# A decode step of attention and MLP on one core: the first tile of wo with seven rows to a partition, the rest of its rows by smaller loads

## The chip, the cores and the metric

The kernel runs on one core of a Trainium2 chip. The metric is the device time of one execution in microseconds; before the change the median of three runs is 393.55 us (393.46 to 393.61). Beside the runs there is one profiled execution, whose instructions, DMA packets and clock were recorded.

## The reference

Eight sequences each decode one token through an attention layer with a cached window and an MLP, both modulated by a condition `c` (adaLN).

```python
B, Sq, D = 8, 1, 512
Hq, Hkv, Sk, Dh = 32, 8, 8192, 128
W = min(4096, max(256, Sk // 4))          # the last 2048 positions of the cache
mod = (_silu(c) @ w_mod).reshape(c.shape[0], 6, 1, -1)
sa, ca, ga, sb, cb, gb = (mod[:, 0], mod[:, 1], mod[:, 2], mod[:, 3], mod[:, 4], mod[:, 5])
h = _layernorm(x) * (1 + ca) + sa
q = (h @ wq) in 32 heads;  k, v = the last W rows of k_cache, v_cache, each for 4 heads
o = softmax(q k^T * Dh ** -0.5) v
x = x + ga * (o.reshape(B, 1, Hq * Dh) @ wo)
h = _layernorm(x) * (1 + cb) + sb
out = x + gb * (relu(h @ w1 + b1) ** 2 @ w2 + b2)
```

All numbers are float32. The K and V windows are 8 x 8 x 2048 x 128 values each, 64 MiB for K and as much for V; wq and wo have 8 MiB each, w_mod 6, w1 and w2 3.5 each.

## The kernel before, in words

Eight key heads are worked off one after the other. For each there are two tiles of keys (four sequences each) and two of values, 4 MiB each: 128 partitions with 32 KiB. A tile goes to one of four big slots (`home`, 128 x 32768 values). A fifth, smaller slot (`small`, 128 x 4096 values, 16 KiB to a partition) takes in turn the second part of w_mod, the first three tiles of wo and the second half of w1.

All large loads are issued by SP, in the order of the list `loads`. A load is issued when a slot of its size is free: `done(key)` frees a slot, and `pump` then goes down the list until the next load finds no slot. The loads are therefore strictly in the order of the list, and on SP's queue a load that waits holds up those behind it.

The steps of the main loop (`for s in range(N + PV_LAG + 1)`, N = 32) are written by hand and set the order on each engine. In a step, VectorE transposes parts of a K tile (`transposes`), TensorE forms scores (`scores`), and five steps behind it multiplies the probabilities with V (`weighted`). `soft_a` to `soft_g` are the softmax of a head, spread over two steps. When a head's values are done, `parts` and `gather` bring its output into columns: `gather` selects with two matmuls against `pick`, transposes, and writes `oT`, 128 x 8 x 32. Two key heads, which are eight query heads, fill `oT` once: head and sixteenth of the head dimension on the partitions (16 h + d // 8), d % 8 in the middle index. Then `project_o(j)` multiplies the eight slices of `oT` with the eight rows that each partition holds of the j-th wo tile (1024 rows), into `wo_ps`, in four column groups of 32 that are added up later. The last of the four wo tiles comes with half of w1 in a big slot (`tail`).

After the loop come the sum over the groups, the residual, the layer norm, w1, the squared ReLU and w2, whose load is cut in four so that its matmuls can follow the pieces. The inputs x and c (`xc`) and the biases come by small loads from ACT's queue. `small` is freed for the second wo tile by `project_o(0)`, at step 14 of the loop.

Of the kernel before, what the change touches and what calls it, by code (L numbers as in the profile page):

```python
# [8 lines left out]
F32 = mybir.dt.float32  # L9
# [10 lines left out]
def tile_adaln_cached_attention_mlp(  # L20
# [14 lines left out]
    nc = tc.nc  # L35
    P = 128
    B, HKV, SK, DH = k_cache.shape
    D = wq.shape[0]
    HQ = wq.shape[1] // DH
    REP = HQ // HKV  # L40
# [12 lines left out]
    consts = ctx.enter_context(tc.tile_pool(name="consts", bufs=1))  # L53
    work = ctx.enter_context(tc.tile_pool(name="work", bufs=2))
    ktp = ctx.enter_context(tc.tile_pool(name="ktp", bufs=2))
    ps_m = ctx.enter_context(tc.tile_pool(name="ps_m", bufs=2, space=bass.MemoryType.PSUM))
# [5 lines left out]
    xc_in = consts.tile([P, 2, P], F32, name="xc_in")  # L62
    x_in, c_in = xc_in[:, 0, :], xc_in[:, 1, :]
    nc.vector.memset(xc_in, 0.0)
    for q in range(D // P):
        b = slice(32 * q, 32 * q + B)
        for x, y in ((0, 2),) if q < 3 else ((0, 1), (1, 2)):
            nc.scalar.dma_start(xc_in[b, x:y], xc[b, x:y])

    ident = consts.tile([P, P], F32, name="ident")  # L70
    make_identity(nc, ident)
# [1 line left out]
    nc.gpsimd.memset(ones, 1.0)  # L73
    eps = consts.tile([P, 1], F32, name="eps")
    nc.vector.memset(eps, EPS)

    big = NJ * DH
# [7 lines left out]
    held = {}  # L87

    def size_of(key):
        return "small" if key[0] in ("wo", "w1") or key == ("mod", 1) else "big"  # L90

    def load(key):
        kind, i = key
        held[key] = free[size_of(key)].pop(0)
        if key == ("wq", 0):
            return
        t = slots[size_of(key)][held[key]]
        if kind in "KV":

            hk, c = divmod(i, 2)  # L100
            v = k_cache[4 * c : 4 * c + 4, hk] if kind == "K" else v_cache[c::2, hk]
            v = v[:, SK - W :, :].rearrange("u (p j) d -> p u (j d)", j=NJ)
            cuts = (0, big // 2, big) if key == ("V", 2 * HKV - 1) else (0, big)
            for x, y in zip(cuts, cuts[1:]):
                nc.sync.dma_start(t[:, x:y], v[..., x:y])
            return

        def rows(o, v):
            n = v.shape[1] * v.shape[2]
            nc.sync.dma_start(t[:, o : o + n].rearrange("p (a n) -> p a n", n=v.shape[2]), v)  # L110

        w1v = w1.rearrange("(p kc) n -> p kc n", p=P)

        def wo_rows(j):

            r = 2 * REP * DH
            v = wo[j * r : (j + 1) * r, :].rearrange("(p i) n -> p (i n)", p=P)
            nc.sync.dma_start(t[:, : big // 2], v)

        if kind == "wo":  # L120
            wo_rows(i)
        elif kind == "mod":

            v = w_mod.rearrange("(p kc) n -> p (kc n)", p=P)
            nc.sync.dma_start(t, v[:, big:] if i else v[:, :big])
        elif kind == "wq":

            o = base[held["wq", 0]]
            nc.sync.dma_start(home[:, o : o + 2 * big], wq.rearrange("(p k) n -> p (k n)", p=P))
        elif kind == "tail":  # L130
            wo_rows(HKV // 2 - 1)
            rows(big // 2, w1v[:, 0:2])
        elif kind == "w1":
            rows(0, w1v[:, 2:4])
        else:
            v = w2.rearrange("(p c) n -> p c n", p=P)
            for lo, hi in ((0, 8), (8, 12), (12, 13), (13, 14)):
                rows(D * lo, v[:, lo:hi])

    def slot(key, n, o=0):  # L140

        t = slots[size_of(key)][held[key]][:, o:]
        return t[:, : t.shape[1] // n * n].rearrange("p (a n) -> p a n", n=n)

    loads = [("mod", 0), ("mod", 1), ("wq", 0), ("wq", 1), ("K", 0), ("K", 1)]
    for n in range(2, 2 * HKV):
        if n in (4, 9, 13):
            loads.append(("wo", n // 4 - 1))
        loads += [("K", n), ("V", n - 2)]
    loads += [("V", 2 * HKV - 2), ("V", 2 * HKV - 1), ("tail", 0), ("w1", 0), ("w2", 0)]  # L150
    at = [0]
# [6 lines left out]
    def done(*keys):  # L158
        for k in keys:
            free[size_of(k)].append(held.pop(k))  # L160
        pump()
# [81 lines left out]
    for k in (2, 3, 4):  # L243
        n = 1 << k
# [134 lines left out]

    def soft_c(hk):  # L380
        pm = MX_.pop(hk)
        m1 = work.tile([1, 4, 32], F32, name="m1")
        nc.vector.tensor_reduce(
            m1.rearrange("p k (u r) -> p k u r", u=4),
            pm[0:1, :P].rearrange("p (u i r) -> p u r i", u=4, i=4)[:, None].to_broadcast([1, 4, 4, 8, 4]),
            axis=AX.X,
            op=ALU.max,
        )
        MX_[hk] = m1
# [78 lines left out]
    def gather(hk):  # L468

        o = OS_.pop(hk)  # L470
        b = slice(H * (hk % 2), H * (hk % 2) + H)
        pp = ps_m.tile([P, 512], F32, name="m_ps", tag="m_ps")
        for x in range(2):
            nc.tensor.matmul(  # L474
                pp[b].rearrange("p (d x e i) -> p x e d i", x=2, e=2, i=8)[:, x],
                pick[:, x].rearrange("p t u -> p (t u)"),
                o.rearrange("p e (d i) -> p e d i", i=8),
                start=True,
                stop=True,
            )  # L480
        tr = work.tile([P, 2, 8, 32], F32, name="tr", tag="b", bufs=1)
        nc.vector.transpose(  # L482
            tr[b].rearrange("p e i (x d) -> p (e i) x d", x=2),
            pp[b].rearrange("p (d x e i) -> p (e i) x d", x=2, e=2, i=8),
        )
        nc.vector.tensor_mul(
            oT[b, :, :B].rearrange("p i (w e) -> p e i w", e=2),
            tr[b, :, :, :4],
            RZ_[hk][b].rearrange("p (w e) -> p e w", e=2)[:, :, None, :].to_broadcast([H, 2, 8, 4]),
        )  # L490

    def project_o(j):

        last = j == HKV // 2 - 1
        key = ("tail", 0) if last else ("wo", j)
        w = slot(key, D)
        for i in range(8):
            nc.tensor.matmul(
                wo_ps[32 * (i % 4) : 32 * (i % 4) + 32, :],
                oT[:, i, :],  # L500
                w[:, i, :],
                start=(j == 0 and i < 4),
                stop=(last and i >= 4),
            )
        if not last:
            done(key)

    def late_tiles():

        late = work.tile([P, NJ, 8, 4], F32, name="pr4", bufs=1).rearrange("p j x w -> p (j x w)")  # L510
        rT = late[:, : FC * 32].rearrange("p (c b) -> p c b", b=32)
        b1_in, b2_in, x1, h2T = late[:NQ, 512 : 512 + FG], late[:NQ, 1024:1152], late[:, 1152:1280], late[:, 1280:1408]
        h2T = h2T.rearrange("p (c b) -> p c b", b=32)
        nc.gpsimd.memset(rT, 0.0)
        for t, v in ((b1_in, b1), (b2_in, b2)):
            v = v.rearrange("(g n) -> g n", g=NQ)
            for g in (0, 2):
                nc.scalar.dma_start(t[g : g + 2], v[g : g + 2])
        return rT, b1_in, b2_in, x1, h2T

    window(0)
# [2 lines left out]
    for s in range(N + PV_LAG + 1):  # L524
        g, i = divmod(s, C)
        q, h = divmod(s, 2)
        v = s - PV_LAG
        soft = 1 <= g <= HKV
        ends = v >= C and v % C == 0
        if i == 1 and soft and g < HKV:  # L530
            soft_e(g - 1)
        if s < N:
            transposes(q, 2 * h, 0)
        if 1 <= s <= N:
            scores((s - 1) // 2, 2 * ((s - 1) % 2) + 1)
            if i == 0:
                soft_a(g - 1)
        if s < N:
            transposes(q, 2 * h, 1)
        if i == 1 and soft:  # L540
            soft_f(g - 1)
        if v > C and v % (2 * C) == 1 and v < N:
            project_o(v // C // 2 - 1)
        if 1 <= v <= N:
            weighted(v - 1, 1)
        if i == 0 and soft:
            soft_b(g - 1)
        if s < N:
            transposes(q, 2 * h + 1, 0)
        if i == 1 and soft:  # L550
            soft_g(g - 1)
            if g == HKV:
                rT, b1_in, b2_in, x1, h2T = late_tiles()
        if i == 0 and soft:
            soft_c(g - 1)
        if 1 <= v <= N and v % 2 == 0:
            parts(v // 2 - 1)
        if s < N:
            scores(q, 2 * h)
        if i == 0 and soft:  # L560
            soft_d(g - 1)
            if g == HKV:
                soft_e(g - 1)
        if s < N:
            transposes(q, 2 * h + 1, 1)
        if 0 <= v < N:
            weighted(v, 0)
        if ends:
            gather(v // C - 1)
# [24 lines left out]

    pa = ps_m.tile([P, 512], F32, name="m_ps", tag="m_ps")
    nc.tensor.matmul(pa[:, 0:1], sel, x1sum, start=True, stop=True)
    xm = work.tile([P, P], F32, name="xm", tag="one_xm", bufs=1)
    nc.vector.tensor_mul(xm, x1, mul)
    nc.vector.tensor_add(xm, xm, add)
    nmean = work.tile([P, 1], F32, name="nmean")  # L600
# [40 lines left out]
    for f in range(FC):  # L641
        for q in range(NQ):
# [4 lines left out]
                start=False,  # L647
                stop=(f == FC - 1),
            )
    y = work.tile([P, P], F32, name="y", tag="one_y", bufs=1)  # L650
    nc.vector.tensor_mul(y, py[:, :P], modC)
    nc.vector.tensor_add(y, y, x1)
    nc.sync.dma_start(out, y)
# [36 lines left out]
```

## Time and profile before

| what | value |
|---|---|
| median of three runs | 393.55 us |
| the profiled execution | 393.74 us |
| its span, first to last instruction | 392.0 us |
| mean granted TensorE clock | 0.887 |
| busy: PE, VectorE (DVE), ACT, POOL | 253.9, 223.8, 46.2, 1.3 us |
| moved by DMA | 165.04 MB, mean 421 GB/s |

Busy time says how long an engine had an instruction in work; PE is TensorE's matmuls, PEld its weight loads, SP the engine that issues the large loads. DMA transfers are carried by 16 DMA engines; a queue (q1 is SP's, q10 ACT's, q8 and q14 bring instructions) is spread over them, and each transfer's rows are packets on them. A share of DMA is the mean over the 16. A row of the waits names who waited, for whom, the total, how often, and the longest. A row of the stretches has the stretch, its length, for each engine the busy time and the number of instructions, then TensorE's granted clock, the DMA share and the rate in GB/s. Times in the timeline and in the chain are from the start of the span.

### The profile page before, as it was taken

What the parts mean: (1) busy time and instruction counts of PE and PEld (TensorE: products, weight loads), DVE (VectorE), ACT (ScalarE), POOL (GpSimd) and SP (SyncE); (2) the same over time, 40 slices, a digit from 0 to 9 for tenths busy, and PEclk for the clock granted to TensorE, in tenths of its full rate; (3) what the DMA queues carried; (4) which work ended last, traced back from release to release, by engine and by line L of the source; (5) the groups of instructions that cost most, each with busy time, mean ns of one, the idle gap of its engine ahead of it and who ended that gap; (6) DMA issues with size and microseconds to landing.
All of it is one profiled execution on the core that took longest, in us unless ns stands there. A gap on an engine that the chain in (4) does not pass through costs nothing.

```text
span 392.0 us, 4698 instructions
## 1 busy us (share of the span) xinstructions
PE 253.9 (65%) x2020; PEld 77.0 (20%) x2020; DVE 223.8 (57%) x314; ACT 46.2 (12%) x89; POOL 1.3 (0%) x8
## 2 busy tenths in 40 slices
PE   0080959868327873797374828893774838996895
PEld 0030300112102221132121202220221211322333
DVE  1261199868057835784583817880786456855231
ACT  0120111310003100310031002010111003004010
POOL 0000000000000000000000000000000000000000
PEclk9996889998959995999698887998697959998999
DMA  8999999999999999999999999999999999999994
GB/s 329 423 468 419 433 431 431 431 430 411 443 428 428 426 428 431 436 435 433 433 430 428 431 430 431 430 428 433 415 441 431 430 431 433 429 416 428 424 420 172
DMA packets 6885, 165.04 MB, mean 421 GB/s; under 512 B 800, under 2 KB 976, under 8 KB 1232
## 3 DMA queue, kind: packets, MB, share of 16 engines
q1 hardware_dynamic: 6768, 164.69, 98.1%
q8 instruction: 16, 0.26, 0.3%
q10 hardware_dynamic: 96, 0.04, 0.0%
q14 instruction: 5, 0.04, 0.0%
HBM read 164.67 MB, written 0.07 MB: 420 GB/s over the span
## 4 chain that ended last, share of the span: by engine, by line
DMA 52%; DVE 23%; PE 19%; issue 4%; ACT 1%; SPq 0%; DVEq 0%; ACTq 0%
DMA home<-in_A_k_cache_dram 37%; DVE kT L191 12%; DMA home<-in_A_wq_dram 9%; PE s_ps L362 6%; DMA home<-in_B_w_dram 6%; DVE pT L428 5%; PE o_ps L448 4%; PE p_ps L393 3%; PE m_ps L307 2%; DVE pr L421 2%; DVE mx L376 1%; PE m_ps L378 1%; DVE qbd L325 1%; PE m_ps L474 1%; PE m_ps L398 1%
## 5 line engine op out<-in xcount | busy, mean ns | idle before, releaser
L191 DVE STREAM_TRANSPOSE kT<-home 128x1024 f32<-128x1024 f32 x128 | 151.5, 1220 | 82.5 <-DMA home<-in_A_k_cache_dram 77.2
L362 PE MATMUL s_ps<-kT,qst 128*32 128x512 f32 x512 | 129.1, 1075 | 21.3 <-DVE kT L191 21.0
L448 PE MATMUL o_ps<-home,pT 128*32 128x256 f32 x1024 | 69.8, 396 | 11.4 <-DVE pT L428 10.5
L448 PEld LDWEIGHTS o_ps<-home,pT 128*32 128x32 f32 x1024 | 33.5, 118 | 105.1 <-issue 65.2
L378 PE MATMUL m_ps<-ident,mx 128*1 128x128 f32 x16 | 4.3, 364 | 59.0 <-DVE mx L376 59.0
L362 PEld LDWEIGHTS s_ps<-kT,qst 128*32 128x32 f32 x512 | 14.2, 116 | 41.6 <-DVE kT L191 32.9
L428 DVE STREAM_TRANSPOSE pT<-pr 128x2048 f32<-128x2048 f32 x8 | 18.2, 2274 | 1.0 <-ACT pr L411 1.0
L411 ACT ACTIVATE pr<-pr,own 128x512 f32<-128x512 f32 x16 | 17.8, 1219 | 0.3
L405 ACT ACTIVATE pr<-p_ps,nm 128x512 f32<-128x512 f32 x8 | 5.5, 689 | 97.6 <-DVE nm L402 97.6
L372 ACT COPY ss<-s_ps 128x512 f32<-128x512 f32 x8 | 4.7, 587 | 101.0 <-issue 73.2
L350 ACT COPY qst<-q_ps 32x128 f32<-32x128 f32 x32 | 8.2, 257 | 70.5 <-PE q_ps L339 70.3
L307 PE MATMUL m_ps<-home,h1T 128*32 128x512 f32 x64 | 8.8, 713 | 9.8 <-DMA home<-in_A_wq_dram 9.8
L225 PE MATMUL m_ps<-xsum,sel 128*128 128x1 f32 x2 | 0.6, 364 | 19.7 <-DVE xsum L223 19.7
L378 PEld LDWEIGHTS m_ps<-ident,mx 128*1 128x1 f32 x16 | 0.7, 81 | 64.2 <-DVE mx L376 64.2
L325 DVE COPY qbd<-m_ps 32x128 f32<-32x128 f32 x8 | 3.0, 371 | 17.1 <-PE m_ps L322 17.0
L393 PE MATMUL p_ps<-ss,perm 128*128 128x512 f32 x16 | 12.5, 872 | 0.0
L402 DVE TENSOR_SCALAR nm<-m_ps 128x1 f32<-128x1 f32 x8 | 1.3, 158 | 17.1 <-PE m_ps L398 17.1
L474 PE MATMUL m_ps<-o_sb,pick 128*64 128x256 f32 x32 | 9.5, 424 | 0.9 <-DVE o_sb L466 0.9
L421 DVE TENSOR_SCALAR pr<-pr,own 128x512 f32<-128x512 f32 x16 | 9.2, 654 | 0.8 <-ACT pr L405 0.8
L203 DVE TENSOR_SCALAR e_sb<-e_sb 128x128 f32<-128x128 f32 x1 | 0.2, 226 | 14.4 <-ACT e_sb L202 14.4
L465 DVE TENSOR_SCALAR o_sb<-o_ps,bit 128x128 f32<-128x128 f32 x16 | 5.2, 328 | 5.3 <-PE o_ps L448 5.1
L482 DVE STREAM_TRANSPOSE tr<-m_ps 64x512 f32<-64x512 f32 x8 | 5.7, 714 | 4.4 <-PE m_ps L474 4.3
(124 smaller groups left out, 119.7 us busy)
## 6 DMA issues: line engine op xcount, KB each, us to landing
home<-in_A_k_cache_dram SPq DMA_DIRECT2D x16, 4096.0 KB, 27.3
home<-in_A_v_cache_dram SPq DMA_DIRECT2D x15, 4096.0 KB, 19.9
small<-in_A_wo_dram SPq DMA_DIRECT2D x3, 2048.0 KB
home<-in_w_mod_dram SPq DMA_DIRECT2D x1, 4096.0 KB, 12.6
home<-in_A_v_cache_dram SPq DMA_DIRECT2D x2, 2048.0 KB, 21.0
small<-in_w_mod_dram SPq DMA_DIRECT2D x1, 2048.0 KB
home<-in_A_wo_dram SPq DMA_DIRECT2D x1, 2048.0 KB, 24.7
home<-in_B_w_dram SPq DMA_DIRECT2D x1, 2048.0 KB
```

Source lines behind the costliest of these rows:

```text
L191: nc.vector.transpose(KTS[q, j][:, rows], k[:, rows, 32 * j : 32 * j + 32])
L307: nc.tensor.matmul(pqs[r][32 * g : 32 * g + 32, :], hT[:, kc, :], w[:, 4 * r + g, :], start=(kc == 0), stop=(kc == NQ - 1),)
L325: nc.vector.tensor_copy(qbd[b, 4 * r : 4 * r + 4, j].rearrange("p g (b t) -> p t g b", t=REP), pT_[b].rearrange("p (t g b) -> p t g b", t= ...
L350: nc.scalar.copy(own[b, :, :, i, 0], pq[b, :P].rearrange("p (c m t) -> p c m t", c=2, t=REP))
L362: nc.tensor.matmul(s_ps[0][32 * g : 32 * g + 32, :], qst[hk % 2][:, P * (4 * c + u) + 32 * j :][:, :32], kT[:, u], start=(c == 0 and j == ...
L378: nc.tensor.matmul(MX_[hk][0:1, :P], mx, ident, start=True, stop=True)
L393: nc.tensor.matmul(sp, perm, SS_.pop(hk), start=True, stop=True)
L411: nc.scalar.mul(X_[hk][..., w], pr, own[:, w : w + 1])
L421: nc.vector.tensor_scalar(X_[hk][..., w], pr, own[:, w : w + 1], None, op0=ALU.mult)
L428: nc.vector.transpose(PT_[hk].rearrange("p e j r -> p j e r"), X_.pop(hk).rearrange("p j x w -> p j (x w)"))
L448: nc.tensor.matmul(O_[n][32 * g : 32 * g + 32, : 2 * DH], PT_[hk][:, e, j : j + 2].rearrange("p j r -> p (j r)"), vt[:, j : j + 2, :].rear ...
L474: nc.tensor.matmul(pp[b].rearrange("p (d x e i) -> p x e d i", x=2, e=2, i=8)[:, x], pick[:, x].rearrange("p t u -> p (t u)"), o.rearrange ...
```

## The change

The first wo tile is cut in two. Of the 128 rows of each of its eight query heads, the first 112 go to the slot at the old place in the list, as seven rows to a partition (`wo_rows(0)`); the head's 16 groups lie on 16 partitions as before. The last 16 rows of each head, 128 rows in all, come with a new load kind `far` into the same slot, where the second wo tile was: 12 of the 16 as four rows each on partitions 32 y + 4 q + a (y the half of the heads, a the head in it, q the group of four rows), by two loads whose outer size is three; the other four, one row each, on every fourth partition from 3. POOL first clears five rows of the slot. The second wo tile moves two places of `n` back in the list.

`gather` puts the outputs of the first two key heads in the order that fits: two matmuls become four. `project_o(0)` multiplies seven slices, and then moves the eighth with four matmuls against `fsel`, a selection matrix made at the start, into `oX`. `far_rows`, at step 18, multiplies the five slices of `oX` with the five rows of `far`. Beside that, the last of the x and c loads is no longer cut in two, each bias comes in one load instead of two, and some working tiles share memory or have one buffer.

```diff
-        for x, y in ((0, 2),) if q < 3 else ((0, 1), (1, 2)):
-            nc.scalar.dma_start(xc_in[b, x:y], xc[b, x:y])
+        nc.scalar.dma_start(xc_in[b], xc[b])
...
+    fsel = consts.tile([P, 4, P], F32, name="fsel")
+    nc.gpsimd.memset(fsel, 0.0)
+    for y in range(2):
+        nc.gpsimd.tensor_copy(
+            fsel[:, :, 32 * y : 32 * y + 12].rearrange("p r (q a) -> p r q a", a=4),
+            ident.rearrange("p (y a r q) -> p y r q a", y=2, a=4, r=4)[:, y, :, :3],
+        )
+    oX = consts.tile([P, 5, 32], F32, name="oX")
...
             r = 2 * REP * DH
+            if j == 0:
+                v = wo[:r].rearrange("(h d) n -> h d n", d=DH)[:, :112].rearrange("h (g i) n -> h g (i n)", i=7)
+                nc.sync.dma_start(t[:, : 7 * D], v)
+                return
...
+        elif kind == "far":
+
+            nc.gpsimd.memset(t[:, : 5 * D], 0.0)
+            v = wo[: 2 * REP * DH].rearrange("(h d) n -> h d n", d=DH)
+            four = v[:, 112:124].rearrange("(y a) (q r) n -> y q a (r n)", y=2, r=4)
+            for y in range(2):
+                nc.sync.dma_start(t[32 * y : 32 * y + 12, : 4 * D], four[y])
+            nc.sync.dma_start(t[3:P:4, 4 * D : 5 * D], v[:, 124:])
...
-        if n in (4, 9, 13):
-            loads.append(("wo", n // 4 - 1))
+        if n == 9:
+            loads.append(("far", 0))
+        if n in (4, 11, 13):
+            loads.append(("wo", (4, 11, 13).index(n)))
...
-        for i in range(8):
+        for i in range(8 if j else 7):
...
+        if j == 0:
+
+            px = ps_m.tile([P, 512], F32, name="m_ps", tag="m_ps")
+            for r in range(4):
+                nc.tensor.matmul(px[:, 32 * r : 32 * r + 32], fsel[:, r], oT[:, 7, :], start=True, stop=True)
+            nc.scalar.copy(oX[:, :4], px[:, :P].rearrange("p (r b) -> p r b", b=32))
+            nc.scalar.copy(oX[:, 4], oT[:, 7, :])
...
+    def far_rows():
+
+        w = slot(("far", 0), D)
+        for r in range(5):
+            nc.tensor.matmul(wo_ps[32 * (r % 4) : 32 * (r % 4) + 32, :], oX[:, r], w[:, r, :], start=False, stop=False)
+        done(("far", 0))
...
-            for g in (0, 2):
-                nc.scalar.dma_start(t[g : g + 2], v[g : g + 2])
+            nc.scalar.dma_start(t, v)
...
+        if s == 18:
+            far_rows()
```

More of the change, by code (lines that the diff above doesn't have):

```diff
@@ L89, in size_of @@
     def size_of(key):
-        return "small" if key[0] in ("wo", "w1") or key == ("mod", 1) else "big"
+        return "small" if key[0] in ("wo", "w1", "far") or key == ("mod", 1) else "big"
     def load(key):
@@ L381, in soft_c @@
         pm = MX_.pop(hk)
-        m1 = work.tile([1, 4, 32], F32, name="m1")
+        m1 = work.tile([1, 4, 32], F32, name="m1", bufs=1)
         nc.vector.tensor_reduce(
@@ L473, in gather @@
         for x in range(2):
[L474 to L480, printed above, removed]
+            to = pp[b].rearrange("p (d x e i) -> p x e d i", x=2, e=2, i=8)[:, x]
+            cuts = [(to, o.rearrange("p e (d i) -> p e d i", i=8))]
+            if hk < 2:
+                cuts = [
+                    (to[..., :7], o[:, :, :112].rearrange("p e (d i) -> p e d i", i=7)),
+                    (
+                        to[..., 7].rearrange("p e (r q) -> p e r q", r=4),
+                        o[:, :, 112:].rearrange("p e (q r) -> p e r q", q=4),
+                    ),
+                ]
+            for dest, src in cuts:
+                nc.tensor.matmul(dest, pick[:, x].rearrange("p t u -> p (t u)"), src, start=True, stop=True)
         tr = work.tile([P, 2, 8, 32], F32, name="tr", tag="b", bufs=1)
@@ L596, in tile_adaln_cached_attention_mlp @@
     nc.tensor.matmul(pa[:, 0:1], sel, x1sum, start=True, stop=True)
-    xm = work.tile([P, P], F32, name="xm", tag="one_xm", bufs=1)
+    xm = work.tile([P, P], F32, name="xm", tag="one_h_sb", bufs=1)
     nc.vector.tensor_mul(xm, x1, mul)
@@ L649, in tile_adaln_cached_attention_mlp @@
             )
-    y = work.tile([P, P], F32, name="y", tag="one_y", bufs=1)
+    y = work.tile([P, P], F32, name="y", tag="one_e_sb", bufs=1)
     nc.vector.tensor_mul(y, py[:, :P], modC)
```

## The prediction

> **What bounds the kernel now.** I read the page first, for the share of each resource; then the chain that ended last and the waits, for who waits for whom; then stretches of the span, for the rate of the transfers and for how they end. Columns of the queue rows: packets, MB, share of 16 engines.
>
> ```profile
> span 392.0 us, 4698 instructions
> ...
> DMA  8999999999999999999999999999999999999994
> ...
> q1 hardware_dynamic: 6768, 164.69, 98.1%
> q8 instruction: 16, 0.26, 0.3%
> q10 hardware_dynamic: 96, 0.04, 0.0%
> ```
>
> SP's queue (q1) keeps the 16 DMA engines busy for 98.1% of the span. No compute engine comes near that. The waits and the last pieces of the chain (start, length, what) agree:
>
> ```profile
> DVE kT L191 <- DMA home<-in_A_k_cache_dram: 77.2, 13, 13.5
> ```
>
> ```profile
> 364.39 22.71 DMA home<-in_B_w_dram
> ...
> 387.15 1.76 PE m_ps L643 x48
> ...
> 388.93 0.30 DVE y L651
> ...
> 389.26 0.29 DVE y L652
> ```
>
> VectorE waits 77.2 us for keys, and the end hangs on the last pieces of w2: when they land, 1.8 us of matmuls, two VectorE operations and the store remain. The time is therefore set by the DMA engine that finishes last. The stretches at the end show that the 16 do not finish together (the last three columns are PE clock, mean busy share of the 16 engines, GB/s):
>
> ```profile
> 384.00:384.50 0.50, 0.00 (x0) 0.00 (x0) 0.00 (x0) 0.00 (x0) 0.00 (x0) 1.00 1.00 397
> 384.50:385.00 0.50, 0.21 (x8) 0.25 (x12) 0.00 (x0) 0.00 (x0) 0.00 (x0) 1.00 0.75 303
> 385.00:385.50 0.50, 0.50 (x28) 0.50 (x24) 0.00 (x0) 0.00 (x0) 0.00 (x0) 1.00 0.60 246
> 385.50:386.00 0.50, 0.50 (x28) 0.50 (x21) 0.00 (x0) 0.00 (x0) 0.00 (x0) 1.00 0.50 205
> ...
> 386.50:387.00 0.50, 0.24 (x11) 0.00 (x0) 0.00 (x0) 0.00 (x0) 0.00 (x0) 1.00 0.50 193
> 387.00:387.50 0.50, 0.35 (x12) 0.35 (x16) 0.00 (x0) 0.00 (x0) 0.00 (x0) 1.00 0.43 164
> 387.50:388.00 0.50, 0.50 (x28) 0.50 (x24) 0.00 (x0) 0.00 (x0) 0.00 (x0) 1.00 0.10 37
> 388.00:388.50 0.50, 0.50 (x22) 0.24 (x16) 0.00 (x0) 0.00 (x0) 0.00 (x0) 1.00 0.13 33
> 388.50:389.00 0.50, 0.36 (x8) 0.09 (x8) 0.07 (x1) 0.00 (x0) 0.00 (x0) 1.00 0.00 0
> ```
>
> The share falls from 1.00 to 0.50 by 385.5 and stays there until 387: eight engines, the early half, are done at about 385.3, and the other eight end up to 388.4. Yet every load of q1 gives all engines the same bytes. What differs is the instruction queue: 0.3% of 16 x 392 us is 18.8 us, or 1.2 us for each of its 16 packets; two on each of eight engines would be 2.4 us, near the lag seen. So at most some 1.5 us (388.4 less the middle of the two ends) can be won by evening out the engines.
>
> **How many engines carry a load.** The counts of packets tell it. q1 has 47 loads and stores of 128 rows, 6016 data packets; the other 752 are 16 per load, one from each engine that closes its part. q10 has five loads of 8 rows and four of 2, 48 data packets, and 48 closing ones: a load with an outer size of 8 or 2 runs on 8 or 2 engines. One engine's rate:
>
> ```profile
> 84.00:124.00 40.00, 23.43 (x190) 6.88 (x186) 20.50 (x24) 4.62 (x9) 0.00 (x0) 0.83 1.00 428
> 124.00:164.00 40.00, 27.27 (x210) 7.87 (x206) 25.73 (x32) 4.63 (x9) 0.00 (x0) 0.87 1.00 430
> 291.00:333.00 42.00, 26.23 (x188) 7.33 (x186) 23.57 (x27) 4.62 (x9) 0.00 (x0) 0.80 1.00 431
> ```
>
> At 430 GB/s an engine moves 26.9 KB (of 1000 bytes) per us.
>
> **The change, part by part.**
>
> The first wo tile moved 131,072 bytes on each of 16 engines, 4.87 us. Now its source view is 8 heads, 16 groups, 3584 values, while the SBUF side still has 128 partitions. Bounds: cut by the source's outer size it runs on 8 engines, 229,376 bytes each, 8.53 us; cut by the partitions, on 16, 114,688 bytes, 4.26 us. I take 8, since an outer size of 8 cannot be dealt out to 16, and q10's loads of 8 rows are the nearest row. The eight get 3.66 us more, the other eight 4.87 us less.
>
> The two loads of outer size three carry 12 pieces of 8192 bytes each. By the same reading three engines move four pieces of each load, 65,536 bytes, 2.44 us (the other bound, 12 engines: 0.61 us). The load on every fourth partition has outer size 8: four pieces of 2048 bytes per engine, 0.30 us.
>
> Sum: the eight get 3.66 + 0.30 = 3.96 us, three of them 2.44 more, 6.40 us; the others lose 4.87 us. Bytes in all are unchanged. Which half the eight are decides the rest, and no view names an engine. I take the early half: where the single packets, which no view prints, can be followed from one's end to the next one's start, q10's lie mostly on chains without instruction packets. That is thin, so the other half keeps a chance. The three then end at 385.3 + 6.40 = 391.7 instead of 388.4, which is **3.3 us later**. If the eight are the late half, it is the whole 6.40 us.
>
> [...]
>
> **Does a late engine's delay reach the end?** Only if the three never run dry.
>
> ```profile
> DMA to landing us min/median/max: 17.2/22.2/35.1
> ```
>
> That row is of the K and V loads. The whole ones take 4,194,304 bytes / 430 GB/s = 9.75 us, so most are issued long before an engine comes to them, 12 us at the median. Issues now move back with landings, by about 3.3 us, but the three engines' own queues by 6.4 us: they stay fed, and the delay is passed on in full. The relieved eight may run dry now and then, at no cost, since they end 8 us early.
>
> **The rest, hidden.** The order on SP, around the second wo tile; rows are line, operation, tiles, the destination's shape and what it waits for. Before:
>
> ```order
> L105 DMA home<-in_A_k_cache_dram 128x1x8192 [waits DMAHW3_49,DVE_49]
> L105 DMA home<-in_A_v_cache_dram 128x1x8192 [waits DMAHW4_49,PE_49]
> L118 DMA small<-in_A_wo_dram 128x4096
> L105 DMA home<-in_A_k_cache_dram 128x1x8192 [waits DMAHW5_49,DVE_49]
> L105 DMA home<-in_A_v_cache_dram 128x1x8192 [waits DMAHW6_49,PE_49]
> ```
>
> After, three loads stand there, behind a wait for POOL, and the tile goes four loads further back:
>
> ```order
> L112 DMA home<-in_A_v_cache_dram 128x1x8192 [waits DMAHW3_49,PE_49]
> L139 DMA small<-in_A_wo_dram 12x1x2048 [waits Pool_49]
> L139 DMA small<-in_A_wo_dram 12x1x2048
> L140 DMA small<-in_A_wo_dram 32x1x512
> L112 DMA home<-in_A_k_cache_dram 128x1x8192 [waits DMAHW4_49,DVE_49]
> ```
>
> All K and V loads behind wait with SP. The rows of before for that place, and the one memset on POOL:
>
> ```profile
> 170.11 1.92 PE L498 MATMUL wo_ps<-small,oT 128*32 128x512 f32 x16
> ...
> 178.82 0.53 SPq L105 DMA_DIRECT2D home<-in_A_v_cache_dram  x1
> ...
> 179.40 0.59 SPq L118 DMA_DIRECT2D small<-in_A_wo_dram  x1
> ...
> 181.15 0.54 SPq L105 DMA_DIRECT2D home<-in_A_k_cache_dram  x1
> ```
>
> ```profile
> 358.57 0.47 POOL L514 MEMSET pr<- 128x448 f32 x1 [357.12 <-DVE pT L428]
> ```
>
> The slot is free at 172.0; a memset of 2560 columns costs 0.47 x 2560/448 = 2.7 us, so POOL is done near 174.7, and SP comes there at 179.4. Two more issues of 0.6 us move the next K load by 1.2 us at most, within the slack above. If the memset took over 7 us, it would begin to eat that slack.
>
> On PE four small matmuls follow the seven of the first tile:
>
> ```order
> L524 MATMUL wo_ps<-small,oT 32x512 [waits DMAHW5_49,DVE_49]
> L524 MATMUL wo_ps<-small,oT 32x512 x6
> L535 MATMUL m_ps<-oT,fsel 128x32 [waits Pool_49]
> L535 MATMUL m_ps<-oT,fsel 128x32 x3
> L469 MATMUL o_ps<-home,pT 32x256 x8
> ```
>
> The eight there were:
>
> ```order
> L498 MATMUL wo_ps<-small,oT 32x512 [waits DMAHW6_49,DVE_49]
> L498 MATMUL wo_ps<-small,oT 32x512 x7
> L448 MATMUL o_ps<-home,pT 32x256 x8
> ```
>
> One fewer in the group, four small ones, five in far_rows and four more in the two gathers are 12 more; eight took 1.92 us, so 3 us in all, below 2 us at one place. PE is busy 27 of 40 us in these stretches, DMA all of them: no cost. Two copies on ACT and the fsel work on POOL hide in the same way. Merging the xc and the bias loads saves three issues on ACT, at places where nothing waits long: no gain. Without that cover it is 3 us, once.
>
> **Rivals.** (a) *Not slower: the first tile stays on 16 engines.* For it: its SBUF side has 128 partitions, like every load of q1. Then all engines save 0.61 us on it, the three end at 385.3 - 0.61 + 2.44 + 0.30 = 387.4, the late half at 387.8, and the time is 392.9. It decides if packets show 16 closers for this load; it would be over 0.2% faster if the late half's instruction packets also cost less, down to 392.0 at most by the 1.5 us above.
>
> (b) *Shared receivers.* The first tile's eight engines now also write partitions that other engines fill at full rate. If a group of partitions takes no more than one engine's 26.9 KB/us, two writers double 8.53 us, three treble it. Two: 8.53 more on the three engines, 396.9 + 8.5 = 405.4. Three, where the far rows add nothing: 385.3 + 3.96 + 17.06 = 406.3, 17.9 later, 411.5. Against it: no row of before shows two engines at one receiver. [...]
>
> (c) *The eight are the late half*: 393.55 + 6.4 = 399.9.
>
> **The numbers.** The profiled execution took 393.74 us, 0.19 above the median of 393.55; the difference is put on the median: 393.55 + 3.3 = **396.9**. Chances: forecast 0.38, (b) 0.27, (c) 0.05, (a) 0.30, of which 0.12 beyond 0.2% faster. So faster 0.12, within 0.2% 0.18, slower 0.70; 0.2%, 0.8 us, is about what a measurement of this kernel can tell from no change. The range runs from 392.6, just under (a), to 406.0, which takes in two writers; three, and a larger gain, are left out, together under 0.2. The forecast's own range is 396 to 398.
>
> **What would show it.** Right: q1 with 6072 data and 758 closing packets (50 transfers; 46 on 16 engines, then 8, 3, 3, 8), 6830 in all; at the end a share of 0.5 before 385, near 0.2 in the last 2 us. (a): 6838 packets and an end like that of before. (b): stretches near 100 to 125 us under 430 GB/s at a share of 1.00, and then a long tail with four engines. Wrong also if the transfers at the end are no longer what the last matmuls wait for.

## The result

The changed kernel took 414.62 us (median of 6 runs, 410.34 to 415.32) against 393.5 us (393.4 to 393.81) for the kernel before in the same rounds: a ratio of 1.0505, interval 1.0454 to 1.0557. That is 21.1 us slower, where 3.3 were predicted. The profiled execution took 414.56 us.

### The profile page after: what moved, and what is told of

It reads as the page before. It is cut to its first block, busy times and chain, and to the rows that moved or that the text cites. A ratio compares the mean times of both kernels' runs of the same rounds, so it can differ in the third digit from the quotient of the medians.

```text
span 412.8 us, 4752 instructions
## 1 busy us (share of the span) xinstructions
PE 257.7 (62%) x2044; PEld 79.7 (19%) x2044; DVE 223.9 (54%) x314; ACT 46.7 (11%) x91; POOL 4.5 (1%) x12
## 3 DMA queue, kind: packets, MB, share of 16 engines
q1 hardware_dynamic: 6830, 164.69, 97.6%
## 4 chain that ended last, share of the span: by engine, by line
DMA 61%; DVE 21%; PE 14%; issue 4%; SPq 0%; ACT 0%; DVEq 0%; ACTq 0%
DMA home<-in_A_k_cache_dram 40%; DVE kT L212 12%; DMA home<-in_A_wq_dram 9%; DMA home<-in_B_w_dram 6%; DMA home<-in_A_v_cache_dram 5%; PE s_ps L383 4%; DVE pT L449 4%; PE p_ps L414 2%; PE m_ps L328 2%; PE o_ps L469 2%; DVE pr L442 2%; DVE mx L397 1%; DVE qbd L346 1%; PE m_ps L399 1%; PE m_ps L419 1%
## 5 line engine op out<-in xcount | busy, mean ns | idle before, releaser
L212 DVE STREAM_TRANSPOSE kT<-home 128x1024 f32<-128x1024 f32 x128 | 151.3, 1220 | 102.3 <-DMA home<-in_A_k_cache_dram 97.3
L328 PE MATMUL m_ps<-home,h1T 128*32 128x512 f32 x64 | 10.0, 797 | 10.9 <-DMA home<-in_A_wq_dram 10.9
L506 PE MATMUL m_ps<-o_sb,pick 128*64 128x256 f32 (+2 forms) x40 | 9.5, 374 | 0.9 <-DVE o_sb L487 0.9
## 6 DMA issues: line engine op xcount, KB each, us to landing
home<-in_A_k_cache_dram SPq DMA_DIRECT2D x16, 4096.0 KB, 36.3
```

Source lines behind the costliest of these rows:

```text
L212: nc.vector.transpose(KTS[q, j][:, rows], k[:, rows, 32 * j : 32 * j + 32])
L328: nc.tensor.matmul(pqs[r][32 * g : 32 * g + 32, :], hT[:, kc, :], w[:, 4 * r + g, :], start=(kc == 0), stop=(kc == NQ - 1),)
L506: nc.tensor.matmul(dest, pick[:, x].rearrange("p t u -> p (t u)"), src, start=True, stop=True)
```

## The profile after

The page of the changed kernel, first its span, the rows of the DMA engines by slices of 10.3 us, and the queues (packets, MB, share of the 16 engines):

```profile
span 412.8 us, 4752 instructions
...
DMA  9999999999999899999999999999999999999993
GB/s 357 459 407 403 453 410 451 413 443 210 154 257 429 365 411 451 419 395 427 426 440 411 422 440 416 446 416 446 416 448 408 451 413 437 414 429 418 428 418 138
...
q1 hardware_dynamic: 6830, 164.69, 97.6%
q8 instruction: 16, 0.26, 0.3%
q10 hardware_dynamic: 80, 0.04, 0.0%
```

The busy share of the DMA engines is as high as before nearly everywhere. The GB/s row is not: in three slices, from about 93 to 124 us, it falls to 210, 154 and 257. The 6830 packets of q1 are the number that the prediction gave for loads on 8, 3, 3 and 8 engines. Stretches of the same kernel around those slices (the last three columns are PE clock, DMA share, GB/s):

```profile
80.00:95.00 15.00, 11.72 (x96) 3.46 (x100) 12.84 (x15) 1.88 (x5) 0.00 (x0) 0.89 0.99 422
95.00:100.00 5.00, 2.36 (x20) 0.35 (x12) 2.75 (x4) 0.00 (x0) 0.00 (x0) 1.00 1.16 185
100.00:105.00 5.00, 3.73 (x40) 1.23 (x40) 0.00 (x0) 0.59 (x1) 0.00 (x0) 1.00 1.10 169
105.00:110.00 5.00, 0.00 (x0) 0.00 (x0) 0.00 (x0) 0.00 (x0) 0.00 (x0) 0.60 0.91 149
110.00:115.00 5.00, 0.00 (x0) 0.00 (x0) 0.00 (x0) 0.00 (x0) 0.00 (x0) 0.50 1.13 176
115.00:120.00 5.00, 0.00 (x0) 0.00 (x0) 0.00 (x0) 0.00 (x0) 0.00 (x0) 0.50 0.83 151
120.00:125.00 5.00, 0.00 (x0) 0.00 (x0) 0.00 (x0) 0.00 (x0) 0.00 (x0) 0.50 0.97 413
125.00:160.00 35.00, 22.06 (x170) 6.68 (x170) 24.72 (x30) 4.05 (x8) 0.00 (x0) 0.83 0.97 411
```

For 25 us all 16 engines count as busy and move 149 to 185 GB/s, then 413 again. All compute engines stand still from 105 to 125 us, and TensorE's granted clock falls in that time from 1.00 to 0.60 and 0.50. The stretch is that of the first wo tile: in the records of the trace, its packets of 14,336 bytes lie from 94.9 to 120.7 us.

The issues of K loads (number, KB each, median us to landing), of the kernel before:

```profile
home<-in_A_k_cache_dram SPq DMA_DIRECT2D x16, 4096.0 KB, 27.3
```

Of the changed kernel, the same row, then the wait for keys and the last pieces of the chain:

```profile
home<-in_A_k_cache_dram SPq DMA_DIRECT2D x16, 4096.0 KB, 36.3
```

```profile
DVE kT L212 <- DMA home<-in_A_k_cache_dram: 97.3, 13, 33.5
```

```profile
382.04 25.84 DMA home<-in_B_w_dram
407.93 1.30 PE m_ps L684 x40
```

VectorE's wait for keys went from 77.2 to 97.3 us, 20.1 more, with the longest single wait 33.5 instead of 13.5. The median time from issue to landing of the K loads is no sign of the delay, though it too went up, from 27.3 to 36.3 us: the kernel below that has no slow stretch and takes 394.2 us shows 36.3 as well. The chain still ends on w2: its pieces land about 20.8 us later (the last group of matmuls starts at 407.93, before at 387.15), which is the growth of the span, 412.8 less 392.0. The end itself, in stretches of 4 us:

```profile
396.00:400.00 4.00, 4.00 (x23) 1.30 (x22) 1.52 (x6) 0.49 (x2) 0.00 (x0) 1.00 0.99 418
400.00:404.00 4.00, 3.91 (x28) 1.69 (x24) 1.68 (x5) 0.27 (x1) 0.00 (x0) 1.00 0.92 384
404.00:408.00 4.00, 2.58 (x70) 1.79 (x72) 0.00 (x0) 0.00 (x0) 0.00 (x0) 1.00 0.50 193
408.00:412.00 4.00, 1.65 (x48) 1.11 (x48) 0.58 (x2) 0.00 (x0) 0.00 (x0) 1.00 0.08 26
```

Between 404 and 408 us the share is 0.50, half of the engines at work. Predicted were four or fewer in a long tail: the other eight were to be done 8 us early. They are not, so they lost time too. POOL's clearing of the slot took about what the prediction gave it (row of the groups of instructions; busy us, mean ns, idle before):

```profile
L135 POOL MEMSET small<- 128x2560 f32 x1 | 2.2, 2232 | 189.5 <-PE wo_ps L524 189.5
```

## The experiments

Two theories stood at the start. **Shared receivers**: several DMA engines write into the same group of partitions, and the group's rate is divided among them (rival b). **The source**: the parts of wo that the eight engines read lie 256 KB apart, and that slows the reads. A third came up on the way: **eight engines** by themselves are the cause. Each diff is against the kernel named ahead of it.

### The first tile alone

Against the changed kernel:

```diff
-        if n == 9:
-            loads.append(("far", 0))
-        if n in (4, 11, 13):
-            loads.append(("wo", (4, 11, 13).index(n)))
+        if n in (4, 9, 13):
+            loads.append(("wo", n // 4 - 1))
...
-        if s == 18:
-            far_rows()
```

> The changed kernel without the far loads and far_rows (128 rows of the sum are left out), the second tile back at its old place; the first tile on eight engines stays. Both theories: the slow stretch of about 25 us near 95 to 120 us stays, the far loads' share (0.3 to 2.7 us) goes: 411 to 414.5 us. If the far loads matter more than that, it falls under 408.

Measured: 414.46 us (414.28 to 414.63), ratio 1.0527 (1.0508 to 1.0546), span 412.5. The loss is in the tile: 414.46 less 393.7 for the kernel before beside it is 20.8 us, and the runs of the changed kernel, 21.1 us slower at the median, lie further apart than the difference. The stretches of this kernel:

```profile
95.00:98.00 3.00, 3.00 (x28) 0.69 (x20) 2.01 (x4) 0.00 (x0) 0.00 (x0) 1.00 1.36 217
98.00:101.00 3.00, 0.55 (x4) 0.00 (x0) 0.97 (x1) 0.00 (x0) 0.00 (x0) 1.00 0.75 115
101.00:104.00 3.00, 2.37 (x20) 1.01 (x24) 0.00 (x0) 0.00 (x0) 0.00 (x0) 0.64 1.11 169
...
115.00:120.00 5.00, 0.00 (x0) 0.00 (x0) 0.00 (x0) 0.00 (x0) 0.00 (x0) 0.50 0.84 152
120.00:125.00 5.00, 0.00 (x0) 0.00 (x0) 0.00 (x0) 0.00 (x0) 0.00 (x0) 0.50 0.98 409
```

They are those of the changed kernel: the far loads and the later second tile have no part in the slow stretch.

### The source at another spacing

Against the kernel with the tile alone; the parts start 113 rows apart instead of 128:

```diff
-                v = wo[:r].rearrange("(h d) n -> h d n", d=DH)[:, :112].rearrange("h (g i) n -> h g (i n)", i=7)
+                v = wo[: 8 * 113].rearrange("(h d) n -> h d n", d=113)[:, :112].rearrange("h (g i) n -> h g (i n)", i=7)
```

> As the run of the tile alone, but the eight parts of the source begin 113 rows (226 KiB) apart instead of 128 rows (256 KiB); the same bytes, eight engines, the same partitions (the rows are the wrong ones). Shared receivers: as the tile alone, within 2 us, with the slow stretch. Sources in step at 256 KiB: the tile runs at full rate, 8.5 us on eight engines, which end 3.7 us later than before's early half: about 394 us, no stretch under 400 GB/s.

Measured: 414.31 us, ratio 1.0523 (1.0504 to 1.0542), span 412.2. Another spacing changes 0.15 us: the source theory falls, as far as the distance of the parts goes.

### The same number of engines, half the bytes, three ways to place them

Three kernels load half of the tile on eight engines, 114,688 bytes on each, and differ only in the partitions and in whether two loads or one fill them. If each engine takes one of the eight outer parts of a load, which is the author's estimate from the counts of packets, an engine fills twice four partitions in the first two and eight in a row in the third. Against the kernel with the tile alone:

```diff
-                nc.sync.dma_start(t[:, : 7 * D], v)
+                for y in range(2):
+                    nc.sync.dma_start(t[32 * y : 32 * y + 32, : 7 * D], v[:, 4 * y : 4 * y + 4])
```

> As the run of the tile alone, but only half of the tile is loaded, by two loads of outer size 8 to 32 partitions each, 0 to 31 and 32 to 63, source parts still 256 KiB apart (half of the tile's rows are left out). [...] Shared receivers: no slow stretch; eight engines carry 4.27 us in place of 4.87, the other eight nothing: the end comes 3 to 3.5 us sooner, 390.0 to 390.6 us. Sources in step: a slow stretch of half the length, about 10 to 12 us, over 400 us.

Measured: 393.62 us (393.41 to 393.86), ratio 1.0 (0.9991 to 1.0009). There is no slow stretch, and no gain of 3 us either; the end of its trace, below, shows why.

The twin of that kernel, the same two loads 64 partitions higher (half of the tile's rows are left out):

```diff
+                    nc.sync.dma_start(t[64 + 32 * y : 96 + 32 * y, : 7 * D], v[:, 4 * y : 4 * y + 4])
```

> [...] Shared receivers: two writers to each of eight groups of partitions for as long as the loads last: the two loads take 8.5 us at half rate, up to 12 us if it is as bad as in the full tile, in place of 4.3; the three engines that end last then end 4 to 7.5 us later than in the twin: 397.5 to 401 us, with 8 to 12 us of a stretch under 350 GB/s. If the number of engines or the source is the cause, or nothing in this form is, it equals the twin: 393.6 us.

Measured: 399.2 us (398.6 to 399.74), ratio 1.0139 (1.0126 to 1.0153), within what shared receivers gave. The stretches of this kernel:

```profile
95.00:98.00 3.00, 3.00 (x28) 0.67 (x20) 2.20 (x4) 0.00 (x0) 0.00 (x0) 1.00 1.25 268
98.00:101.00 3.00, 1.62 (x24) 0.68 (x24) 0.78 (x1) 0.00 (x0) 0.00 (x0) 1.00 0.86 178
101.00:104.00 3.00, 2.47 (x24) 0.54 (x16) 0.00 (x0) 0.59 (x1) 0.00 (x0) 1.00 1.05 245
```

One load to partitions 0 to 63 instead of two:

```diff
+                nc.sync.dma_start(t[:64, : 7 * D], v[:, :8])
```

> The same half of the tile, the same partitions 0 to 63 as in the first of these twins, the same rows and eight engines, but in one load of outer size 8 with eight rows for each (half of the tile's rows are left out). [...] Shared receivers: the eight run at half rate, 8.5 us in place of 4.3, the other eight are not touched: about 397 to 398 us, and the DMA rate in the stretch falls to some 325 GB/s (eight at half rate, eight at full). If the other eight slow down too, what is shared is not the receiver alone. [...]

Measured: 398.37 us (398.3 to 398.45), ratio 1.0119 (1.01 to 1.0137), a little over what was expected.

Stretches of the kernel with two loads to partitions 0 to 63, in the middle and at the end:

```profile
95.00:98.00 3.00, 3.00 (x36) 0.79 (x32) 2.73 (x4) 0.00 (x0) 0.00 (x0) 1.00 1.08 462
98.00:101.00 3.00, 3.00 (x32) 0.75 (x24) 0.00 (x0) 0.59 (x1) 0.00 (x0) 1.00 1.05 446
101.00:104.00 3.00, 0.01 (x2) 0.00 (x0) 0.00 (x0) 0.00 (x0) 0.00 (x0) 1.00 0.98 415
104.00:107.00 3.00, 0.00 (x0) 0.00 (x0) 0.00 (x0) 0.00 (x0) 0.00 (x0) 0.64 1.02 437
...
384.00:386.00 2.00, 2.00 (x50) 1.27 (x52) 0.20 (x1) 0.00 (x0) 0.00 (x0) 1.00 0.38 151
386.00:388.00 2.00, 1.58 (x60) 1.31 (x52) 0.00 (x0) 0.00 (x0) 0.00 (x0) 1.00 0.18 61
```

Of the kernel with one load to the same partitions:

```profile
95.00:98.00 3.00, 3.00 (x28) 0.65 (x20) 2.43 (x4) 0.00 (x0) 0.00 (x0) 1.00 1.17 252
98.00:101.00 3.00, 1.61 (x24) 0.68 (x24) 0.56 (x1) 0.00 (x0) 0.00 (x0) 1.00 1.00 224
101.00:104.00 3.00, 2.25 (x24) 0.55 (x16) 0.00 (x0) 0.59 (x1) 0.00 (x0) 1.00 0.94 226
104.00:107.00 3.00, 0.00 (x0) 0.00 (x0) 0.00 (x0) 0.00 (x0) 0.00 (x0) 0.97 0.95 371
```

The number of engines, the bytes and the source are the same in all three, and the first moves 415 to 462 GB/s from 95 to 107 us, its twin 178 to 268 and the third 224 to 252 from 95 to 104 us. So it is the placement that decides, where rival (b) looked for the loss. In the kernel with two loads to partitions 0 to 63 the tile's packets took 0.54 us, in its twin on partitions 64 to 127 1.11 us, and in the one load to partitions 0 to 63 1.09 us, each time with the other eight engines loading keys. Which partitions an engine fills in the loads of keys is not shown; the expected times rest on an assumption of the author's. The last two rows of the kernel with two loads to partitions 0 to 63 are its end: a share of 0.18, about three engines of 16, from 386 to 388. The other eight have 4.87 us less to carry, so three of the tile's eight must be among the late ones, and they hold the end where it was. Why these three, with 0.6 us less to carry themselves, do not end a little sooner is not shown.

What neither theory expected is the size of the rate. The kernel with one load to partitions 0 to 63 was to move some 325 GB/s, with the eight engines of the tile at half rate and the other eight untouched. It moved 224 and 226, half of everything. The single DMA packets in the records of the traces, which no view prints, say the same (median us, with the number of packets: all of the tile, and those of 32,768 bytes that start and end while the tile is being loaded):

| kernel | packets of the tile | packets of 32,768 bytes beside them |
|---|---|---|
| before | 0.61 (128, of 16,384 bytes) | 1.21 (15) |
| half tile, two loads, partitions 0 to 63 | 0.54 (64, of 14,336 bytes) | 1.22 (40) |
| half tile, two loads, partitions 64 to 127 | 1.11 (64) | 2.41 (41) |
| half tile, one load, partitions 0 to 63 | 1.09 (64) | 2.30 (30) |
| changed kernel | 1.58 (128) | 3.28 (60) |

The large packets belong to K loads, which have the form that they have in the kernel before. In the middle of each load on eight engines, 8 packets of the tile and 8 large ones are in flight at a time, so the large ones are those of the other eight engines. They slow down about as much as the tile's: by two in the slow half tiles, by 2.7 in the changed kernel, where the tile's packets take 2.9 times as long as at full rate.

How many engines write into a group of partitions at a time is an estimate: if a group's rate is divided evenly, 0.54, 1.11, 1.09 and 1.58 us stand for one, two, two and three writers. No view names an engine or the partition of a packet, so neither the groups nor their writers are seen. Why the K packets, at 2.30 to 3.28 us instead of 1.21, slow down with the tile's is not shown.

### The whole tile in two loads of 64 partitions

Against the kernel before; the first tile in two loads of 64 partitions, with all rows:

```diff
+            if j == 0:
+                for y in range(2):
+                    nc.sync.dma_start(t[64 * y : 64 * y + 64, : big // 2], v[64 * y : 64 * y + 64])
+                return
```

> The kernel before with its first tile, all 1024 rows, in two loads of 64 partitions each, outer size 64 on both sides, so that 16 engines carry each of them; nothing is left out. [...] Shared receivers: 9.7 us for the tile on all engines in place of 4.9: 398.4 us, and more if it is as bad as in the full tile on eight engines. If the small number of engines is the cause: no change, 393.5 to 394 us.

Measured: 400.66 us (400.26 to 402.06), ratio 1.0185 (1.0166 to 1.0203). Stretches of this kernel:

```profile
95.00:98.00 3.00, 2.20 (x16) 0.26 (x8) 2.58 (x4) 0.00 (x0) 0.00 (x0) 1.00 1.19 235
98.00:101.00 3.00, 1.41 (x16) 0.72 (x20) 0.00 (x0) 0.00 (x0) 0.00 (x0) 0.77 0.92 202
101.00:104.00 3.00, 3.00 (x32) 0.86 (x24) 0.00 (x0) 0.56 (x1) 0.00 (x0) 0.66 1.04 213
104.00:107.00 3.00, 0.19 (x4) 0.00 (x0) 0.00 (x0) 0.02 (x1) 0.00 (x0) 0.91 1.06 235
107.00:110.00 3.00, 0.00 (x0) 0.00 (x0) 0.00 (x0) 0.00 (x0) 0.00 (x0) 0.50 0.86 306
```

From 95 to 107 us they show 202 to 235 GB/s, with the bytes of the kernel before: half the rate again. The tile's 128 packets of 1.27 us at the median are some 163 us, 11 at a time in the 15 us of these stretches, where the loads on eight engines had 8 at a time; that 16 engines carry each load is not shown. With eight engines at full rate in the half tile on partitions 0 to 63 (0.54 us a packet), the number of engines is not the cause; that theory falls. These five stretches of 3 us moved 3.57 MB where 430 GB/s would have moved 6.45; 2.88 MB at 430 GB/s are 6.7 us, the loss of 6.9 (400.66 less 393.73 beside it) but for 0.2.

One more rival is that an engine is slow because it writes other partitions than in the loads around the tile, not because two write into one group. No run here tells the two apart. All 128 packets of the tile are slow, 0.70 us at the least, where the kernel before has 0.61 at the median and 0.62 at the most.

### The rest of the change without the slow tile

Against the changed kernel; the tile's source is cut so that all 16 engines carry it, seven rows each:

```diff
-                v = wo[:r].rearrange("(h d) n -> h d n", d=DH)[:, :112].rearrange("h (g i) n -> h g (i n)", i=7)
+                v = wo[:r].rearrange("(p i) n -> p (i n)", p=P)[:, : 7 * D]
```

> The changed kernel, but the first tile's source is cut as 128 rows of 3584 values (the first seven of every eight rows of wo), so that both outer sizes are 128; the far loads and all the rest stay. The rows are then the wrong ones for the sums, the work is the same. Both theories (receivers shared by several engines; sources 256 KiB apart read in step) put the loss on the first tile's load on eight engines: no slow stretch, 430 GB/s throughout, three engines carry 2.4 us more, the others 0.6 us less: 392.9 us, 392.4 to 393.6. If the far loads, the later place of the second tile or POOL's memset cost the time, it stays above 400 us.

Measured: 394.22 us (394.07 to 394.39), ratio 1.0011 (1.0002 to 1.002); q1 has 6838 packets. All other parts of the change, the far loads, the matmuls, POOL's clearing and the selection, cost 0.5 us together. The gain that rival (a) gave this case, down to 392.9, is not there. Three kernels test where it went. The merged x, c and bias loads alone, in the kernel before:

```diff
-        for x, y in ((0, 2),) if q < 3 else ((0, 1), (1, 2)):
-            nc.scalar.dma_start(xc_in[b, x:y], xc[b, x:y])
+        nc.scalar.dma_start(xc_in[b], xc[b])
...
-            for g in (0, 2):
-                nc.scalar.dma_start(t[g : g + 2], v[g : g + 2])
+            nc.scalar.dma_start(t, v)
```

> The kernel before with only the merged loads of the change: x and c in four loads instead of five, each bias in one instead of two; nothing is left out. The prediction held them for neutral: 393.5 to 393.9 us. If the 16-engine version's missing gain (394.2 instead of 392.9) comes from them, because three fewer loads shift which semaphore a later load waits for: 394.3 to 394.8 us.

Measured: 393.82 us (393.7 to 394.02), ratio 1.0 (0.999 to 1.0011): no cost and no gain.

The tile of seven rows on 16 engines without the far loads; against the kernel that has both:

```diff
-        if n == 9:
-            loads.append(("far", 0))
-        if n in (4, 11, 13):
-            loads.append(("wo", (4, 11, 13).index(n)))
+        if n in (4, 9, 13):
+            loads.append(("wo", n // 4 - 1))
...
-        if s == 18:
-            far_rows()
```

> The kernel after with the first tile as seven rows on 16 engines (114,688 bytes on each instead of 131,072), without the far loads and far_rows, and with the second tile at its old place; 128 rows of wo are left out. Theory A, the end is set by what the late engines carry: every engine has 16,384 bytes less, 0.61 us at 26.9 KB/us, so 393.7 - 0.6 = 393.1 us, and the run with the far loads (394.2) then shows that these cost about 1.1 us by themselves. Theory B, what an engine saves in the middle of the kernel is not seen at the end: 393.7 as before, and the far loads cost about 0.5 us.

Measured: 393.68 us (393.48 to 393.98) against 393.6, ratio 1.0001 (0.9992 to 1.001).

And the far loads with the whole tile on 16 engines, against the same kernel:

```diff
-                v = wo[:r].rearrange("(p i) n -> p (i n)", p=P)[:, : 7 * D]
-                nc.sync.dma_start(t[:, : 7 * D], v)
+                v = wo[:r].rearrange("(p i) n -> p (i n)", p=P)
+                nc.sync.dma_start(t[:, : 8 * D], v)
```

> The kernel after with all eight rows of the first tile loaded on 16 engines as before, seven of them used, and with the far loads, far_rows and the later place of the second tile; the products of the other rows are not the reference's. It carries 262,144 bytes more than before, all on the engines of the far loads. Theory A, the saving in the tile counts in full and the far loads cost about 1.1 us: 393.7 + 1.1 = 394.8 us. Theory B, the saving does not count: 394.2, as with the seven rows.

Measured: 394.82 us (394.67 to 395.2) against 393.6, ratio 1.0031 (1.002 to 1.0043). The end of this kernel:

```profile
387.50:388.00 0.50, 0.36 (x15) 0.09 (x4) 0.00 (x0) 0.00 (x0) 0.00 (x0) 1.00 0.79 283
388.00:388.50 0.50, 0.20 (x8) 0.20 (x12) 0.00 (x0) 0.00 (x0) 0.00 (x0) 1.00 0.45 168
388.50:389.00 0.50, 0.50 (x28) 0.50 (x24) 0.00 (x0) 0.00 (x0) 0.00 (x0) 1.00 0.13 49
```

The answers do not fit one theory. With the far loads, the eighth row on all engines costs 0.60 us (394.82 less 394.22; 0.70 when each is taken against the kernel before beside it), near the 0.61 worked out from its bytes. Without them, taking it away brings nothing (393.68 against 393.6). So the far loads cost 1.2 us beside a full tile and some 0.5 beside a shorter one. With them more engines are still at work near the end, a share of 0.79 after 387.5 us where the kernel before had 0.10, which says that engines of the early half have become late ones.

Part of that cost is again slower packets. Near the far loads, some 50 packets of 32,768 bytes take 1.25 to 1.42 us instead of 1.22, in both kernels that have these loads on top of a fast tile; the excess adds up to about 6 us, or 0.4 us for each of 16 engines.

Why the late half does not end sooner with 16,384 bytes less to carry stays open. In the timeline of the kernel with seven rows and no far loads (start, busy us, line and operation, idle before and its releaser) the second piece of w2 is there at 387.19 us, as against 387.15 before:

```profile
387.19 1.74 PE L680 MATMUL m_ps<-home,pr 128*32 128x128 f32 x48 [0.43 <-DMA home<-in_B_w_dram]
```

One difference in its queues may bear on that. Between 386 and 388.05 us this kernel has an instruction packet:

```profile
q8 instruction: 1, 0.02, 2.8%
```

The same stretch has one in the two kernels with far loads on a fast tile and in the half tile at full rate, and none in the kernel before or in the one with the merged loads, where the last such packet comes at 388.4 and 388.1 us, after the last packets of w2. It takes one engine 0.9 to 1.4 us. Whether that engine is one that ends last is not shown.

No version here beats the kernel before; the merged loads and the shorter tile are level with it.

## Why the prediction was wrong

**How many engines: right.** q1 has 6830 packets, the number for 8, 3, 3 and 8, and 8 packets of the tile are in flight at a time.

**At what rate: this step failed.** The prediction let each of the eight engines move 229,376 bytes at 26.9 KB/us, in 8.53 us, since the nearest rows show an engine at that rate. But those rows do not have this placement, and the experiments say that the placement sets the rate. The tile's packets took 1.58 us instead of 0.54, and its load 25.7 us (94.9 to 120.7); 8.53 us at a third of the rate are 25.6. Rival (b) put the loss in the right place and had a chance of 0.27, yet its case of three writers, 411.5 us, was left out of the range, and even that fell short of 414.6. No run shows its term, a group of partitions that takes no more than one engine's 26.9 KB/us and has two or three writers; the expected times of the experiments rest on it too. What the runs showed in its place are packets of 1.09 and 1.11 us in the slow half tiles and of 1.58 us in the whole tile, instead of 0.54.

**What the other eight lose: not seen by any case.** Forecast and rival (b) let them gain 4.87 us. At a third of the rate for 25 us they lose some 16.7 us (an estimate from the 3.28 us of their packets) and gain 4.87, about 12 in all; that is why half of the engines still work at 404 to 408 us instead of four.

**Which half: wrong in part.** The eight were taken for the early half. In the half tile at full rate (two loads, partitions 0 to 63) the other eight engines have 4.87 us less to do, and from 386 to 388 us three engines are left of the eight that the kernel before shows at work until 387: three of the tile's eight belong to the late ones. That is worked out from shares and not seen on single engines. Counted from the late end, the sum at a third of the rate is 25.6 - 4.87 + 0.30 = 21.0 us; counted from the early one, rival (b) had 17.9. Measured were 21.1. The forecast's own terms, so corrected, would have come to 393.55 + 3.96 = 397.5, if the three engines of the far loads are not among the late ones.

**Does the delay reach the end: right.** The 20.7 us that the tile takes longer (25.6 less 4.87) are in the wait for keys (20.1 more), in the landing of w2 (20.8 later) and in the time.

**The far loads: wrong in size.** On the early half they were to end at 385.3 + 2.74 = 388.0, under the late half and at no cost beside a full tile; they cost 1.2 us there. The slower packets beside them are about 0.4 of it; where the rest comes from was not settled.

**The hidden rest: right.** POOL's 2.2 us (2.7 predicted), the merged loads (ratio 1.0) and the matmuls do not show; the kernel that has them all without the slow tile is at 1.0011.

**Rival (a)** had its packets in the experiment on 16 engines, 6838 as it said, but not its time: 394.2 instead of 392.9.

## What to carry to other kernels

When a load is cut in a new way, ask not only how many DMA engines carry it but also which partitions it fills, and in what parts. Here packets of 16,384 bytes took 0.61 us in the load of 128 partitions with an outer size of 128, and 1.27 us in two loads of 64 partitions. Packets of 14,336 bytes took 0.54 us in two loads of outer size 8 to partitions 0 to 63, but 1.11 us in the same two loads to partitions 64 to 127, 1.09 us in one load of outer size 8 to partitions 0 to 63, and 1.58 us in the one to all 128. Look for it in the GB/s of a stretch, not in the busy share, which here stayed at 0.83 to 1.16 while the rate fell from 422 GB/s to 149 to 185. Bound the price by all 16 engines at the slowed rate, for as long as the load takes; for the engines that carry the load, that is its whole time at that rate less what it took before (here 25.6 less 4.87, of 21.1 measured).

## What the runs showed of the hardware that was not expected

- While a slow tile was loaded, the packets of other loads were slow too: those of 32,768 bytes of the K loads took 2.30 and 2.41 us beside the slow half tiles and 3.28 us beside the whole one, instead of 1.21. The rates over the core were 178 to 268 GB/s (95 to 104 us) and 149 to 185 (95 to 120 us) instead of about 430. How many engines write at a group of partitions is an estimate from these times, not seen.
- Two loads of 64 partitions instead of one of 128, with the same bytes, cost 6.9 us for a tile of 2 MB (ratio 1.0185, interval 1.0166 to 1.0203).
